# A gated feed-forward block on one core: two down blocks made earlier, one staged tile placed apart, and a set of x sums reordered

## The chip, the cores and the metric

The kernel runs on one core of a Trainium2 chip. The time is device microseconds of that core; the median of three runs before the change is 541.72 us (541.16 to 542.87). The engines are TensorE (PE, with PEld for its weight loads), VectorE (DVE), ScalarE (ACT), GpSimd (POOL) and SyncE (SP), which issues nearly every transfer here, in one queue and in order. One further execution was taken by the profiler: 542.6 us, of which the span from the first to the last instruction is 540.8 us. Places in time below are microseconds from the start of that span.

## What is computed

Input x is 2048 x 1024, w_gate and w_up are 1024 x 3584, w_down is 3584 x 1024, all in bf16:

```python
g = jnp.einsum("bsd,df->bsf", x, w_gate)
u = jnp.einsum("bsd,df->bsf", x, w_up)
h = _gelu(g) * u
return jnp.einsum("bsf,fd->bsd", h, w_down)
```

The kernel doesn't multiply these matrices block by block. It uses a Strassen-like scheme with seven products for eight on 2 x 2 blocks, for the gate and up products and for the down product, and for some units a second level of it. The price is sums and differences of blocks: of x (the t sums), of the weights (the s sums) and of w_down (the "down blocks" m). They are worked out on VectorE, ScalarE and GpSimd beside TensorE's matmuls.

## The kernel before the change

**Passes and units.** The 2048 rows of x are taken in two passes (ip 0 and 1) of 1024. A pass has 14 units, u = 0 to 13, of 256 columns of w_gate and w_up each. Units 1 to 3, 12 and 13 of pass 0 go through `unit` (L238). Units 4 to 11 go two at a time: `pair0` (L357) in pass 0 (a = 4, 6, 8, 10) and `pair1` in pass 1. Behind the units of a pass comes the down stage, `down` (L630).

**Banks.** The eight PSUM banks are four pairs, passed around as roles F, K, E, C. In `unit` the roles are `e, c, d = banks`; in `prepare` and `keep` the pair K is the one that a unit's helper work may use. A product is summed up in a bank by TensorE (L132), copied out by ScalarE (`snap`, L125: u2, p1, p5), and added to others by VectorE (`dve`, L108: sums, "up" sums, then the product of `gelu` (L200) and up, written to hT or hL).

**Order.** The instructions of SP, VectorE, GpSimd and TensorE run in the order of the code, so the order is written by hand; an instruction that waits holds up all behind it on its engine. ScalarE's are in code order within the blocks that a manual schedule marks, which hold the units.

**Rotating places.** `slot` (L97) hands out one of 36 places of 2 KB per partition (kpool) or one of 13 for s sums (spool). wpool has three places of 8 KB for the weight tiles W(u) of a unit and for other big tiles; mpool has two for down blocks (`three`, L100). A new tile in a place waits until all readers of the old one are done, a DMA among them.

**Down blocks.** For each j of 14, three differences of blocks of w_down are made once, in pass 0, stored to DRAM (`store_made`, L534: 768 KB) and loaded in both down stages. Two ways exist. `keep_part` (L512), in three parts: ScalarE casts a piece into a spare bank, VectorE subtracts from it (one bank, one SBUF input). `keep_whole` (L526): three subtractions on GpSimd. Before, `JS` (L62) gives each pair two blocks by parts, ja at its start and jb at its end (blocks 0 to 7); unit 12 makes block 8 and unit 13 block 9 by parts; GpSimd makes 10, 11 (in `prepare` of unit 12), 12 and 13 (of unit 13). `fetch_wd` (L501) loads the raw pieces: two slots for j up to 9, a w place for two blocks from 10 on. The stores of blocks 10 and 11 are issued in unit 13, those of 12 and 13 at the down stage's steps 0 and 2 (`more`, L964).

**The staged outputs.** Nine 512-wide pieces of h in pass 0 have no place yet when they are made, because `forms` lies where hL will be. Eight go to a w place (`staged`, t8), the ninth to a slot named hx (L865). `bring_home` (L346), in pair 10, copies them to hL by two DMAs.

**The x sums of the second level.** `lo_part` (L826) makes T1, T2, T3, T4, TB (in `forms`) from x, in unit 2 for k = 0 and unit 3 for k = 1. Parts 0 to 2 are called in `keep`, part 3 by `turned`, behind the product with s3. While `turned` is set, `unit` adds p5 to the banks of e in place and takes it off again behind the last product (L287).

**The down stage.** `raw[1, n]` holds raw w_down pieces for the first 28 products; four are fetched ahead in unit 13 (L934), the others by the agenda, step by step. Then the stored down blocks follow (`load12`, `load4`).

Of the kernel before, what the change touches and what calls it, by code (L numbers as in the profile page):

```python
# [10 lines left out]
def kernel(  # L11
# [26 lines left out]
    P = nc.NUM_PARTITIONS  # L38
    bf16 = mybir.dt.bfloat16
# [19 lines left out]
    NWARM = 7  # L59
    SLOTS, SUMS = 36, 13  # L60
    FIRST, LAST = 4, 11
    JS = {4: (0, 1), 6: (2, 3), 8: (4, 5), 10: (6, 7)}  # L62
    LAG = 3
    BIG12 = (0, 2, 4)
    AT12 = [6, 6, 10, 10, 14, 14, 16, 18, 20, 22, 27, 29, 31, 33]
# [169 lines left out]
        for i in range(2):  # L235
            nc.scalar.copy(out=ps[i], in_=src[i])

    def unit(u, banks, s, t, late, after_p5, aside, keep, ahead_of_p4, behind_p4, turned):  # L238
        GU = range(2)
        e, c, d = banks  # L240
        aside(-2)
        g, up = late() if late else (None, None)
        aside(-1)
        for i in GU:
            product(e[i], s["s2"][i], t["t2"], False)
        aside(0)
        keep(0, c)
        u2 = [snap(e[i], "u2") for i in GU]
        if late:
            g = gelu(g)  # L250
        c11 = g, up
        keep(1, c)
        keep(2, c)
        c = d
        for i in GU:
            product(c[i], s["s1"][i], t["t1"], True)
        p5 = [snap(c[i], "p5") for i in GU]
        after_p5()
        for i in GU:
            product(e[i], s["s3"][i], t["t3"], False)  # L260
        if turned and u % 2:
            turned(banks[1])
        elif turned:
            g, up = add(e, p5)
            times(2 * u + 1, 1, gelu(g), up)
            turned(banks[1])
        else:
            g, up = new(dve, e[0], p5[0], ADD, "sum", dtype=f32), banks[1][not late]
            dve(up, e[1], p5[1], ADD)
        if late:  # L270
            times(2 * u, 0, *c11)
        for i in GU:
            product(c[i], s["s4"][i], t["tb"], False)
        if not turned:
            times(2 * u + 1, 1, gelu(g), up)
        aside(1)
        g, up = add(c, u2)
        times(2 * u, 1, gelu(g), up)
        if turned and u % 2:
            g, up = add(e, p5)  # L280
            times(2 * u + 1, 1, gelu(g), up)
        ahead_of_p4()
        for i in GU:
            product(e[i], s["sa"][i], t["t4"], False)
        behind_p4()
        if turned:
            dve(e[1], e[1], p5[1], SUB)  # L287
        times(2 * u + 1, 0, gelu(e[0]), e[1])


# [1 line left out]
    T1, T2, T3, T4, TB = [[forms[:, 2 * n + i] for i in range(2)] for n in range(5)]  # L292
    pd = dpool.tile([P, LAST - FIRST + 1, 2, N], f32, name="pd")
    st8 = []

    def staged(n, c):
        if not st8:
# [59 lines left out]
    def pair0(a, roles, S, t, js, hooks):  # L357
# [16 lines left out]
        sb.make("s4")  # L374

        def keep(j, n, ps):
            keep_part(j, n, ps[n % 2])

        ja, jb = js
        hooks("w", n)  # L380
        keep(ja, 0, K)
        full(F, sa["s2"], t["t2"])
# [19 lines left out]
        hadd(E, u2a, 2 * a, 1)  # L402
        part(K, q["r3"], T3, False)
        squared(F, p5a, 2 * a + 1)
        part(E, q["r1"], T1, True)
        sb.make("sa")
        hooks("w", nn)
# [1 line left out]
        full(C, sb["s3"], t["t3"])  # L409
        for i in range(2):  # L410
            dve(A[i], K[i], p5r[i], ADD)
        part(E, q["r4"], TB, False)
        hooks("pd", b)
        part(K, [x[:, H:] for x in sb["s1"]], T4, False)
        hooks("home", b)
        for i in range(2):
            dve(B[i], E[i], u2r[i], ADD)
        hooks("pd", a)
        hooks("fetch", a)
        p5b = [snap(K[i], "p5") for i in range(2)]  # L420
        raw1(F, W(n))
# [78 lines left out]

    def fetch_wd(js):  # L501
        for j in js:
            if j < NJ - 4:
                wraw[j] = [slot([P, Dm], bf16, "raw") for _ in range(2)]
            else:
                if j % 2 == 0:
                    big = wpool.tile([P, 4, Dm], bf16, name="w")
                wraw[j] = [big[:, 2 * (j % 2) + kh] for kh in range(2)]
            for kh in range(2):
                nc.sync.dma_start(out=wraw[j][kh], in_=wdn[:, kh, j, :])  # L510

# [13 lines left out]

    def keep_whole(j):  # L526
        ra, rb = wraw[j]
        made[j] = wpool.tile([P, 4, N], f32r, name="w") if j in (NJ - 3, NJ - 2) else three(f32r)
        m = [made[j][:, n] for n in range(3)]
        pool(m[0], ra[:, N:], ra[:, :N], SUB)  # L530
        pool(m[1], rb[:, N:], m[0], SUB)
        pool(m[2], rb[:, :N], m[1], SUB)
# [265 lines left out]

    def making(u):
        if u == NU - 2:  # L800
            return [8]
        return [9, 10, 11, 12, 13] if u == NU - 1 else []

    E, K, C, F = odd, cc, dd, even
    S, p5 = {}, {}
# [20 lines left out]
    def lo_part(k, part, c):  # L826
        t1 = t["t1"]
        if part == 0:
            nc.scalar.copy(out=c[0], in_=lo[:, KH + k])
            dve(c[0], c[0], lo[:, k], SUB)  # L830
        if part == 1:
            nc.scalar.copy(out=c[1], in_=lo[:, KH + H + k])
            dve(TB[k], c[1], lo[:, H + k], SUB)
            dve(T3[k], TB[k], c[0], SUB)
        if part == 3:
            dve(c[0], c[0], t1[k], SUB)
            dve(c[1], TB[k], c[0], SUB)
            dve(T4[k], t1[H + k], c[1], SUB)
            nc.scalar.copy(out=T1[k], in_=c[0])
            nc.scalar.copy(out=T2[k], in_=c[1])  # L840

# [5 lines left out]
    for ip in range(NPASS):  # L847
        with tc.manual_schedule(engines={ENG.Activation}):
# [6 lines left out]
            for u in range(1 if ip == 0 else 0, NU):  # L855
                if upgraded(u):
                    if u % 2:
                        continue
                    if u == FIRST:
                        S = {u: s, u + 1: sums_s(W(u + 1), pool)}  # L860
                    if (ip, u) == (0, FIRST):
                        for n in range(4):
                            for c in range(2):
                                away[NH + n, c] = lambda n=n, c=c: staged(n, c)
                        away[NH + 4, 0] = lambda: slot([P, N], bf16, "hx")  # L865

                    def hooks(what, n):
                        if what == "w":
                            W(n)
                            if ip == 0 and n - 3 in JS:  # L870
                                fetch_wd(JS[n - 3][1:])
                            if ip and n <= LAST:
                                fetch_p5(n)
                        if what == "home" and n == LAST:
                            bring_home()
                        if what == "pd":
                            k = 0 if n % 2 else KH
                            nc.sync.dma_start(
                                out=pd[:, n - FIRST].rearrange("p i n -> p (i n)"),
                                in_=flat(xT[1][:, k : k + KH]),  # L880
                            )
                        if what == "made":
                            store_made(n)
                        if what == "fetch":
                            fetch_wd(JS.get(n + 2, [8, 10, 11])[: 1 if n + 2 in JS else 3])

                    roles = F, C, K, E
                    if ip == 0:
# [10 lines left out]
                def prepare():  # L899
                    if first:  # L900
                        pool_behind(t["t4"][-1])
                    if u + 1 < NU:
                        nxt["s"] = make_s(W(u + 1), pool, nxt.get("s"))
                    if ip == 0:
                        if js:
                            store_made(js[0])
                        if u == NU - 2:
                            for j in making(u + 1)[1:3]:
                                keep_whole(j)
                        if u == NU - 1:  # L910
                            for j in js[3:]:
                                keep_whole(j)
                        if u == FIRST - 2:
                            fetch_wd(JS[FIRST][:1])

                def keep(part, ps):
                    if js:
                        keep_part(js[0], part, ps[part // 2])
                    if ip == 0 and u in (2, 3):
                        lo_part(u - 2, part, ps)  # L920

                def aside(part):
                    if first and part < 0:
# [5 lines left out]
                        if (ip, u) == (0, 1):  # L929
                            load_lo()  # L930
                    if part == 0 and (ip, u) == (0, NU - 2):
                        fetch_wd([9, 12, 13])
                    if part == 0 and (ip, u) == (0, NU - 1):
                        for n in range(4):  # L934
                            fetch12(n)
                            ahead12.add(n)
                        for j in js[1:3]:
                            store_made(j)
                    if part == 0 and "t4" not in t:
                        t.make("t4")  # L940

# [9 lines left out]
                if u % 2 and not first:  # L951
                    E, K, C = C, E, K
                banks = (E, K, C) if u % 2 else (F, K, E)
                turned = (lambda c: lo_part(u - 2, 3, c)) if ip == 0 and u in (2, 3) else None
                unit(
                    u, banks, s, t, late if first else None, prepare, aside, keep,
                    ahead_of_p4, behind_p4, turned,
                )
                s = nxt.pop("s", None)

# [3 lines left out]
        def more(step):  # L964
            if last:
                return
            if step in (0, 2):
                store_made({0: NJ - 2, 2: NJ - 1}[step])
            if step == 0:
                xT[:] = new_x()  # L970
            if step >= 24 and step % 2 == 0 and step // 2 - 12 < len(moves):
# [43 lines left out]
```

## Time and profile before

| what | value |
|---|---|
| median of three runs | 541.72 us (541.16 to 542.87) |
| the profiled execution | 542.6 us |
| its span | 540.8 us, 7482 instructions |
| granted TensorE clock | 1.000 |
| transfers | 103.91 MB, mean 192 GB/s |
| HBM read, written | 78.64 MB, 19.40 MB |

How to read it: "busy" is the time in which an engine ran instructions, beside its share of the span. A row such as `out<-in xcount` groups instructions by the tiles they write and read. The bracket behind a row of the timeline is the time for which the engine sat idle before it and the instruction or transfer that ended the wait last, inferred from semaphores. SPq rows are the issues of transfers, and their duration is that of issuing, not of moving data. Busy times by stretch (us, then PE, PEld, DVE, ACT, POOL, granted clock, DMA share of 16 engines, GB/s):

```profile
40.00:64.00 24.00, 23.69 (x107) 16.83 (x107) 20.59 (x32) 16.73 (x32) 23.98 (x23) 1.00 0.34 98
64.00:94.00 30.00, 29.93 (x134) 22.05 (x134) 20.86 (x32) 20.86 (x39) 23.59 (x26) 1.00 0.43 132
94.00:122.00 28.00, 27.93 (x126) 20.34 (x126) 20.82 (x33) 20.16 (x38) 23.97 (x25) 1.00 0.69 207
150.00:178.00 28.00, 26.89 (x120) 19.43 (x120) 18.17 (x29) 17.66 (x34) 23.39 (x23) 1.00 0.83 278
178.00:200.00 22.00, 19.89 (x84) 14.99 (x83) 16.65 (x26) 14.27 (x28) 15.31 (x14) 1.00 0.86 307
200.00:226.00 26.00, 25.47 (x116) 11.87 (x118) 21.51 (x33) 2.58 (x6) 2.12 (x2) 1.00 1.12 370
```

The first stretch holds units 2 and 3, the second and third pairs 4 and 6, the fourth pair 10, the fifth units 12 and 13, the last the beginning of the down stage. GpSimd's last instruction of pass 0 is in that last stretch.

### The profile page before, as it was taken

The page shows a single profiled execution, that of the slowest core. Times are in us where ns is not written, and L with a number is a line of the kernel's source. Part 1 is how long each engine was busy: PE and PEld are TensorE (multiplying, and loading weights), DVE is VectorE, ACT ScalarE, POOL GpSimd, SP SyncE. Part 2 cuts the span into 40 slices and gives each one's busy share as a digit, 9 for nine tenths or more (in the row PEclk, how much of TensorE's full clock was granted, in tenths as well). Part 3 has the DMA queues.
Part 4 walks back from the last instruction along what each step waited for, and adds up shares of the span by engine and source line. Part 5 has one row for each costly group of instructions (what it writes and reads, how often), then busy time and mean ns, then how long its engine had stood idle before and what let it go on. Part 6 is the DMA issues. An engine that isn't in the chain of part 4 may idle for free.

```text
span 540.8 us, 7482 instructions
## 1 busy us (share of the span) xinstructions
PE 531.4 (98%) x2372; PEld 377.5 (70%) x2393; DVE 363.4 (67%) x564; ACT 276.2 (51%) x497; POOL 269.0 (50%) x253
## 2 busy tenths in 40 slices
PE   9999999999999999999999999999999999999997
PEld 5568686868686664588886867668667685488886
DVE  2987867777775879658587455576675749775830
ACT  3557676868683741015345645656666551104351
POOL 1079986979798480000006949793979620000000
PEclk9999999999999999999999999999999999999999
DMA  9795063946769799989995443343561239655571
GB/s 245 174 232 167 1 175 117 279 150 196 233 196 320 252 388 365 337 253 216 259 322 151 122 137 99 115 120 113 160 189 28 57 102 383 235 175 161 170 240 53
DMA packets 115527, 103.91 MB, mean 192 GB/s; under 512 B 21792, under 2 KB 97696, under 8 KB 115360
## 3 DMA queue, kind: packets, MB, share of 16 engines
q1 hardware_dynamic: 115488, 103.44, 64.4%
q8 instruction: 19, 0.31, 0.3%
q14 instruction: 20, 0.16, 0.1%
HBM read 78.64 MB, written 19.40 MB: 181 GB/s over the span
## 4 chain that ended last, share of the span: by engine, by line
PE 89%; DMA 4%; DVE 3%; ACT 2%; issue 1%; SPq 0%; DVEq 0%; ACTq 0%
PE bank L132 89%; DMA raw<-in_w_down_dram 2%; DMA hL<-hx 1%; DVE bank L108 1%; DMA xn<-in_x_dram 1%; ACT g L200 1%; DVE hT L108 1%; DVE forms L108 0%; DVE sum L108 0%; DVE m L108 0%; DVE hL L108 0%; ACT bank L519 0%; SPq L707 0%; ACT forms L840 0%; ACT u L125 0%
## 5 line engine op out<-in xcount | busy, mean ns | idle before, releaser
L111 POOL TENSOR_TENSOR s<-w 128x512 fp32r<-128x512 bf16 x102 | 120.2, 1194 | 138.7 <-PE bank L132 107.5
L132 PE MATMUL bank<-t,s 128*128 128x512 f32 x552 | 132.1, 392 | 1.0 <-DVE m L108 0.7
L132 PEld LDWEIGHTS bank<-t,s 128*128 128x128 f32 x552 | 103.5, 188 | 23.9 <-DVE m L108 1.1
L132 PE MATMUL bank<-xT,w 128*128 128x512 bf16 (+1 forms) x489 | 108.0, 376 | 2.3 <-DMA raw<-in_w_down_dram 0.9
L132 PEld LDWEIGHTS <-w 128*128 128x128 bf16 x504 | 47.8, 98 | 60.0 <-issue 6.6
L200 ACT ACTIVATE g<-sum 128x512 f32<-128x512 f32 x81 | 51.5, 635 | 65.9 <-DVE sum L108 60.0
L125 ACT COPY p<-bank 128x512 f32<-128x512 f32 x102 | 57.7, 590 | 50.0 <-PE bank L132 50.0
L108 DVE TENSOR_TENSOR sum<-bank,p 128x512 f32<-128x512 f32 x54 | 37.1, 687 | 38.1 <-PE bank L132 37.0
L108 DVE TENSOR_TENSOR hT<-g,bank 128x512 bf16<-128x512 f32 x72 | 49.1, 687 | 16.3 <-ACT g L200 9.9
L111 POOL TENSOR_TENSOR s<-w,s 128x512 fp32r<-128x512 bf16 x50 | 57.9, 1174 | 0.9 <-PE bank L132 0.6
L111 POOL TENSOR_TENSOR s<-s,w 128x512 fp32r<-128x512 f32 x50 | 57.4, 1164 | 0.4
L132 PE MATMUL bank<-tb,s 128*128 128x512 f32 x216 | 54.4, 394 | 1.2 <-ACT p L125 1.2
L132 PE MATMUL bank<-t,sa 128*128 128x512 f32 x216 | 55.1, 397 | 0.0
L120 ACT CAST tb<-raw 128x512 fp32r<-128x512 bf16 x28 | 17.5, 630 | 73.4 <-PE bank L132 30.3
L108 DVE TENSOR_TENSOR bank<-bank,p 128x512 f32<-128x512 f32 x72 | 49.8, 695 | 7.4 <-PE bank L132 7.4
L132 PE MATMUL bank<-q 128*128 128x512 f32 x208 | 51.7, 389 | 0.0
L132 PEld LDWEIGHTS bank<-tb,s 128*128 128x128 f32 x216 | 40.4, 188 | 10.5 <-POOL w L111 1.5
L132 PEld LDWEIGHTS bank<-t,sa 128*128 128x128 f32 x216 | 40.6, 188 | 9.1
L132 PEld LDWEIGHTS bank<-q 128*128 128x128 f32 x208 | 39.0, 188 | 8.1
L125 ACT COPY u<-bank 128x512 f32<-128x512 f32 x56 | 32.1, 594 | 15.7 <-PE bank L132 15.7
L132 PE MATMUL bank<-raw,hT 128*128 128x512 bf16 x140 | 31.2, 379 | 0.2
L108 DVE TENSOR_TENSOR q<-raw 128x512 fp32r<-128x512 bf16 x28 | 19.2, 687 | 17.9 <-DMA raw<-in_w_down_dram 10.3
(80 smaller groups left out, 636.1 us busy)
## 6 DMA issues: line engine op xcount, KB each, us to landing
raw<-in_w_down_dram SPq DMA_DIRECT2D x72, 256.0 KB, 5.1
w<-in_w_gate_dram SPq DMA_DIRECT2D x27, 512.0 KB, 4.7
w<-in_w_up_dram SPq DMA_DIRECT2D x27, 512.0 KB, 5.9
q<-td SPq DMA_DIRECT2D x52, 256.0 KB, 4.4
td<-m SPq DMA_DIRECT2D x12, 768.0 KB, 5.3
w<-td SPq DMA_DIRECT2D x6, 1024.0 KB, 9.8
pd<-xT SPq DMA_DIRECT2D x8, 512.0 KB, 4.6
out_dram<-st SPq DMA_DIRECT2D x32, 128.0 KB, 1.9
```

Of the source, the lines that this page charges most:

```text
L108: nc.vector.tensor_tensor(out=out, in0=a, in1=b, op=op)
L111: nc.gpsimd.tensor_tensor(out=out, in0=a, in1=b, op=op)
L120: nc.scalar.copy(out=t, in_=src)
L125: nc.scalar.copy(out=t, in_=ps)
L132: nc.tensor.matmul(ps, lhsT=lhs, rhs=rhs, start=start, stop=stop, skip_group_check=True)
L200: nc.scalar.activation(g, src, ACT.Gelu_apprx_tanh)
```

## The change

- `JS` and a new `MID`: pairs 4 and 6 make a third block each, by parts, in their middle (blocks 1 and 4); pairs 8 and 10 make 6, 7 and 8, 9; unit 12 makes 10 and unit 13 makes 11, by parts.
- GpSimd makes 12 and 13 alone, both in `prepare` of unit 12, into w places; their stores are issued in unit 13 and at step 0 of the down stage.
- The raw pieces of blocks 1 and 4 come into one w place, loaded ahead of pair 4; those of 12 and 13 into another, as before.
- hx has a place of its own in xpool.
- In units 2 and 3, parts 0 and 1 of the x sums are both made in the first `keep`, part 2 (three VectorE steps, split off from part 3) in the last, and part 3 (the two copies to T1 and T2) in `prepare`. `turned` is gone from `unit`: the up sum is written to the other bank pair as in other units, and the subtraction behind the last product falls away.

The order of TensorE's instructions is the same in both. VectorE has four instructions more (six block subtractions more, two subtractions less), ScalarE six more, GpSimd six fewer; SP issues the same transfers in another order.

```diff
-    JS = {4: (0, 1), 6: (2, 3), 8: (4, 5), 10: (6, 7)}
+    JS = {4: (0, 2), 6: (3, 5), 8: (6, 7), 10: (8, 9)}
+    MID = {4: 1, 6: 4}
+    BIGS = (1, 4, 12, 13)
...
-        if turned and u % 2:
-            turned(banks[1])
-        elif turned:
-            g, up = add(e, p5)
-            times(2 * u + 1, 1, gelu(g), up)
-            turned(banks[1])
-        else:
-            g, up = new(dve, e[0], p5[0], ADD, "sum", dtype=f32), banks[1][not late]
-            dve(up, e[1], p5[1], ADD)
+        g, up = new(dve, e[0], p5[0], ADD, "sum", dtype=f32), banks[1][not late]
+        dve(up, e[1], p5[1], ADD)
...
-        if turned and u % 2:
-            g, up = add(e, p5)
-            times(2 * u + 1, 1, gelu(g), up)
...
-        if turned:
-            dve(e[1], e[1], p5[1], SUB)
...
+    hx = xpool.tile([P, N], bf16, name="hx")
...
         ja, jb = js
+        jm = MID.get(a)
...
         squared(F, p5a, 2 * a + 1)
+        keep(jm, 0, F)
         part(E, q["r1"], T1, True)
...
             dve(A[i], K[i], p5r[i], ADD)
+        keep(jm, 1, F)
+        keep(jm, 2, F)
         part(E, q["r4"], TB, False)
...
         hooks("pd", a)
+        if jm is not None:
+            hooks("made", jm)
         hooks("fetch", a)
...
-            if j < NJ - 4:
+            if j not in BIGS:
                 wraw[j] = [slot([P, Dm], bf16, "raw") for _ in range(2)]
...
-        made[j] = wpool.tile([P, 4, N], f32r, name="w") if j in (NJ - 3, NJ - 2) else three(f32r)
+        made[j] = wpool.tile([P, 4, N], f32r, name="w")
...
         if u == NU - 2:
-            return [8]
-        return [9, 10, 11, 12, 13] if u == NU - 1 else []
+            return [10]
+        return [11] if u == NU - 1 else []
...
-        if part == 3:
+        if part == 2:
             dve(c[0], c[0], t1[k], SUB)
             dve(c[1], TB[k], c[0], SUB)
             dve(T4[k], t1[H + k], c[1], SUB)
+        if part == 3:
             nc.scalar.copy(out=T1[k], in_=c[0])
             nc.scalar.copy(out=T2[k], in_=c[1])
...
                     if (ip, u) == (0, FIRST):
+                        fetch_wd(MID.values())
...
-                        away[NH + 4, 0] = lambda: slot([P, N], bf16, "hx")
+                        away[NH + 4, 0] = lambda: hx
...
-                            fetch_wd(JS.get(n + 2, [8, 10, 11])[: 1 if n + 2 in JS else 3])
+                            fetch_wd(JS[n + 2][:1] if n + 2 in JS else [10, 12, 13])
...
+                    if ip == 0 and u in (2, 3):
+                        lo_part(u - 2, 3, K)
                     if u + 1 < NU:
                         nxt["s"] = make_s(W(u + 1), pool, nxt.get("s"))
...
-                            for j in making(u + 1)[1:3]:
-                                keep_whole(j)
-                        if u == NU - 1:
-                            for j in js[3:]:
+                            for j in BIGS[2:]:
                                 keep_whole(j)
...
                     if ip == 0 and u in (2, 3):
-                        lo_part(u - 2, part, ps)
+                        for n in ((0, 1), (), (2,))[part]:
+                            lo_part(u - 2, n, ps)
...
-                        fetch_wd([9, 12, 13])
+                        fetch_wd([11])
...
-                        for j in js[1:3]:
-                            store_made(j)
+                        store_made(BIGS[2])
...
-            if step in (0, 2):
-                store_made({0: NJ - 2, 2: NJ - 1}[step])
+            if step == 0:
+                store_made(BIGS[3])
```

More of the change, by code (lines that the diff above doesn't have):

```diff
@@ L236, in into, with unit @@
             nc.scalar.copy(out=ps[i], in_=src[i])
-    def unit(u, banks, s, t, late, after_p5, aside, keep, ahead_of_p4, behind_p4, turned):
+    def unit(u, banks, s, t, late, after_p5, aside, keep, ahead_of_p4, behind_p4):
         GU = range(2)
@@ L273, in unit @@
             product(c[i], s["s4"][i], t["tb"], False)
-        if not turned:
-            times(2 * u + 1, 1, gelu(g), up)
+        times(2 * u + 1, 1, gelu(g), up)
         aside(1)
@@ L278, in unit @@
         times(2 * u, 1, gelu(g), up)
-        if turned and u % 2:
-            g, up = add(e, p5)
-            times(2 * u + 1, 1, gelu(g), up)
         ahead_of_p4()
@@ L376, in keep @@
         def keep(j, n, ps):
-            keep_part(j, n, ps[n % 2])
+            if j is not None:
+                keep_part(j, n, ps[n % 2])
         ja, jb = js
+        jm = MID.get(a)
         hooks("w", n)
@@ L502, in fetch_wd @@
         for j in js:
-            if j < NJ - 4:
+            if j not in BIGS:
                 wraw[j] = [slot([P, Dm], bf16, "raw") for _ in range(2)]
             else:
-                if j % 2 == 0:
+                n = BIGS.index(j) % 2
+                if n == 0:
                     big = wpool.tile([P, 4, Dm], bf16, name="w")
-                wraw[j] = [big[:, 2 * (j % 2) + kh] for kh in range(2)]
+                wraw[j] = [big[:, 2 * n + kh] for kh in range(2)]
             for kh in range(2):
@@ L953 @@
                 banks = (E, K, C) if u % 2 else (F, K, E)
-                turned = (lambda c: lo_part(u - 2, 3, c)) if ip == 0 and u in (2, 3) else None
                 unit(
                     u, banks, s, t, late if first else None, prepare, aside, keep,
-                    ahead_of_p4, behind_p4, turned,
+                    ahead_of_p4, behind_p4,
                 )
```

## The prediction

> **What bounds the kernel now.** I read the clock per core first (1.000 over the whole span, so nothing is throttled), then the page's busy times.
>
> ```profile
> span 540.8 us, 7482 instructions
> PE 531.4 (98%) x2372; PEld 377.5 (70%) x2393; DVE 363.4 (67%) x564; ACT 276.2 (51%) x497; POOL 269.0 (50%) x253
> ```
>
> TensorE is the bound, and the change leaves its instructions and their order as they are. So only its idle time can change: 540.8 - 531.4 = 9.4 us. Of that 3.2 us lie behind the last matmul (it ends at 537.6), 1.25 us in the first 20 us (18.75 busy), and about 1.3 us in gaps of 0.07 us that most stretches of 20 us show alike. The rest is in the waits of TensorE:
>
> ```profile
> PE bank L132 <- DMA raw<-in_w_down_dram: 1.3, 3, 0.9
> PE bank L132 <- ACT p L125: 1.2, 1, 1.2
> PE bank L132 <- DVE m L108: 0.7, 1, 0.7
> PE bank L132 <- ACT u L125: 0.2, 1, 0.2
> PE bank L132 <- DVE hT L108: 0.2, 1, 0.2
> ```
>
> TensorE's timeline tells where they stand (start, duration, and in brackets the idle time before and what ended it):
>
> ```profile
> 63.33 1.02 PE L132 MATMUL bank<-xT,w 128*128 128x512 bf16 x4 [0.24 <-DVE hT L108]
> ...
> 176.00 3.02 PE L132 MATMUL bank<-xT,w 128*128 128x512 bf16 x12 [0.93 <-DMA raw<-in_w_down_dram]
> ...
> 181.59 2.10 PE L132 MATMUL bank<-t,s 128*128 128x512 f32 x8 [0.71 <-DVE m L108]
> 183.94 2.06 PE L132 MATMUL bank<-t,s 128*128 128x512 f32 x8 [0.25 <-ACT u L125]
> ...
> 196.43 2.07 PE L132 MATMUL bank<-tb,s 128*128 128x512 f32 x8 [1.16 <-ACT p L125]
> ...
> 221.26 1.89 PE L132 MATMUL bank<-raw,hL 128*128 128x512 bf16 x7 [0.21 <-DMA raw<-in_w_down_dram]
> ```
>
> With a last one of 0.16 us at 223.31 these are 3.66 us: 0.24 in unit 3, 1.89 between the last pair and unit 12, 1.16 in unit 13, 0.37 where the down stage begins. Behind 230 us TensorE waits for nothing. Four lines of ScalarE and VectorE show what stands behind the middle ones:
>
> ```profile
> 174.59 0.63 ACT L200 ACTIVATE g<-sum 128x512 f32<-128x512 f32 x1 [4.63 <-DMA hL<-hx]
> 175.25 0.69 DVE L108 TENSOR_TENSOR hL<-g,bank 128x512 bf16<-128x512 f32 x1 [3.36 <-ACT g L200]
> 193.94 0.69 DVE L108 TENSOR_TENSOR m<-bank,raw 128x512 fp32r<-128x512 f32 x1 [2.77 <-issue]
> 194.67 1.11 ACT L519 CAST bank<-raw 128x512 f32<-128x512 bf16 x2 [2.34 <-DVE m L108]
> ```
>
> **The change, part by part.** Times of steps are added from rows: a VectorE subtraction or product lasts 0.69 us and starts 0.60 after the one before it, 0.73 if it reads that one's result; ScalarE's gelu lasts 0.63, its copy 0.59, with 0.5 between starts.
>
> *The staged tile (hx).* A gelu output g takes the rotating place that hx had, so ScalarE waits 4.63 us until hx has been copied home. The product of that g ends at 175.25 + 0.69 = 175.94, and TensorE starts at 176.00 in the bank it read: this is the 0.93 (the row names a DMA, but these matmuls read no raw tile). With a place of its own, g follows its sum: VectorE did the second half of that addition at 171.20, so g runs at 171.3 and its product ends at 172.7, well ahead of 175.07, where TensorE would need the bank. Then the rest of the in-order chain: addition 172.65 and 173.25, g 173.4, product 174.1 to 174.8, subtraction to 175.4, product to 176.1, then three block subtractions at 176.1, 177.3 and 178.0, the last ending at 178.7. TensorE, 0.93 earlier, wants that bank at about 179.8 (before: 180.9, and 181.59 when it got it). So 0.71 goes with 1.1 us to spare. Next: sum 178.6, g 179.4, a cast to 180.5, the two u copies to 181.0 and 181.5, wanted at 181.8 and 182.7: 0.25 goes with 0.8 to spare. Together 1.89; bounds: 0 if another wait stands in the same place, 1.89 if none.
>
> *Two down blocks fewer on GpSimd at the end, two more in pairs 4 and 6.* In unit 13 block 9's first subtraction stands 2.77 us behind GpSimd's use of the m buffers and a store that took 7.5 us (issued 186.31); the next cast waits for it (194.67), then the p copies, then TensorE: 1.16. Now unit 13 makes block 11, whose m buffer is freed by the store of block 9, issued as block 9 is done, about 178.8; at 4.3 to 8.2 us for such stores (issues of 181.56 to 190.24) it lands by 187.0. The subtraction would want to start about 189.2. The raw data of block 11 come behind that store: issue 179.2 to 180.5, 4.6 us, landed by 185.1, wanted by ScalarE at 188.3. So 1.16 goes; bounds 0 and 1.16.
>
> GpSimd made four blocks from 185.98 to 202.2, with two waits for m buffers; two blocks of 3.7 us, straight after its last s sum (184.1, now 183.2), end near 190.6. SP's queue stood behind it: the store at 202.22 and then a burst of thirteen transfers. From 200 to 220 the DMA share is 1.03 at 374 GB/s, and the last raw transfer, issued at 212.41, took 10.85 us. Two stores (2 x 768 KB) leave this region, and the one at 202.22 can go out near 194: three stores, 2.3 MB, at 374 GB/s are 6 us of transfers less in it, against TensorE's arrival 3.3 us earlier. So the 0.37 goes too (bounds 0 and 0.37, and a loss, see the rivals).
>
> *Price of the middle blocks.* Six casts on ScalarE (590 ns) and six subtractions on VectorE (690 ns), half in pair 4, half in pair 6, into bank pair F, which is idle between its last product and the next raw product. In pair 4:
>
> ```profile
> 77.74 1.15 ACT L120 CAST sa<-w 128x512 fp32r<-128x512 bf16 x2
> 83.08 1.07 ACT L125 COPY p<-bank 128x512 f32<-128x512 f32 x2 [2.61 <-PE bank L132]
> 78.84 0.69 DVE L108 TENSOR_TENSOR hT<-g,bank 128x512 bf16<-128x512 f32 x1
> 83.51 3.40 PE L132 MATMUL bank<-xT,w 128*128 128x512 bf16 x15
> ```
>
> The first cast goes ahead of the sa casts (77.8), subtraction 79.4; sa casts to 79.4; p5 copies to 80.5; A additions 80.1 and 80.7; casts two and three to 81.6; subtractions 81.3 and 82.0, ending at 82.7. TensorE takes F at 83.51: 0.8 us to spare. VectorE's B additions slip from 82.1 to 82.6, the next sum from 83.7 to 83.8, and the product that follows waited 1.43 us anyhow. I take 0. The cover is this 0.8 us; once it is gone, each further us late costs one in each pair, and the raw product of F, its p1 copies and the unit's sums are late behind it.
>
> Here the Trainium skill speaks against the change. "Perfetto Trace Analysis", section "Optimizing Scalar/DVE Operations", warns that moving work between GpSimd and VectorE might not help, since they share a read port; "SBUF — State Buffer", section "Who interferes with whom", limits this to VectorE instructions with two SBUF inputs. These have one (the other is PSUM), and the row agrees: the block subtraction at 96.84 took 0.68 us inside a GpSimd run from 96.30 to 98.59. By the limited rule and the row the price is 0; by the warning taken broadly it is the third rival's.
>
> *The big tile for blocks 1 and 4* holds one of three w places from 48 us to the middle of pair 6. SP's order puts its four loads ahead of W(6), which now waits for W(4)'s last reader, the raw product ending at 60.7; W(7) waits for the sa casts of pair 4, 79.5 instead of 72.2. Two places are what pair 8 has now, as t8 holds the third:
>
> ```profile
> 134.72 0.37 SPq L142 DMA_DIRECT2D w<-in_w_gate_dram  x1
> ...
> 146.16 3.63 PE L132 MATMUL bank<-xT,w 128*128 128x512 bf16 x16
> ```
>
> Its W(11) goes out 11.4 us ahead of its first matmul, lands 5.3 us after issue, and TensorE doesn't wait. One pair is 27.87 us, so pairs 4 and 6 repeat this some 0.5 us later (the extra cast). GpSimd's s1, s2 of unit 7 end near 90.1, wanted at 97. I take 0, by pair 8; at the slowest landing seen (10.85) W(7) would come at 90.8, wanted at 90.4, and W(9) likewise: bounds 0 and 0.8 lost. The extra store goes out behind the pd stores and delays the next raw fetch by some 2 us of 11.
>
> *x sums in units 2 and 3.* Two subtractions go (2 x 0.69), the T1, T2 copies come ahead of the sa casts, and the up sum goes to the second K bank once T2 is copied. Unit 2: both casts by 41.5, six form steps on VectorE from 41.4 to 45.5, T2 copied at 46.1, e sum 45.4 (before 45.35), up sum 46.2 (46.26), the c sum 48.3 instead of 49.73, as no form step stands ahead of it. Unit 3: casts 50.2 and 50.7, six form steps 51.0 to 55.1, e and up sums 55.0 and 55.6, c sums 57.3 and 57.9, their product to 59.4, then the raw sums at 60.0 and, when the bank is ready, 60.8, gelu to 61.3, product 61.5 to 62.2. Before, the chain was back to back on VectorE to 63.28; TensorE wants that bank at 63.1. So 0.24 goes, with 0.9 to spare at the tightest u2 copy (52.3, wanted at 53.2). Bounds: 0.24 gained to nothing.
>
> **Sum.** 0.24 + 1.89 + 1.16 + 0.37 = 3.66 us, 0 added: 542.6 (the profiled execution, 1.8 us more than its span) becomes 538.9. The median of the runs shown is 541.72, 0.9 below it. If those runs hold the same waits they come to 538.1; if their waits are that much shorter, to 538.9. I take the middle, 538.5.
>
> **Rivals.** (1) The waits don't go but change hands: hx is free, yet the same bank waits for the copies, or unit 13 waits for store 9. For: margins of 0.8 to 1.8 us against stores that vary by 4. Then only about half is won: 541.72 - 1.9 = 539.8, at worst 541. Against: each margin is as large as the wait it replaces.
> (2) The down stage takes it back: TensorE arrives 3.3 us earlier at transfers that land as before, and waits 3.3 more at 219 to 223: 541.7. For: 374 GB/s there. Against: GpSimd's end, 11 us earlier, was what held SP.
> (3) Slower: in pairs 4 and 6 each of three subtractions is blocked by a running GpSimd instruction (1.15 us each), so F is 3.45 - 0.8 = 2.65 us late in each pair, 5.3 in all: 541.72 - 3.66 + 5.3 = 543.4. It decides from 0.8 + 3.66 / 2 = 2.6 us late in each pair on: there the gain is eaten. Against: the 0.68 us row.
>
> **How the numbers follow.** Forecast 0.70, rival 1 0.14, rival 2 0.08, rival 3 0.08. The forecast's own range is 537.3 (538.1 less the runs' 0.8) to 539.6. Rival 1 fills 539.6 to 541; to leave out no more than 2 in 10 the range goes to 541.2. About 0.3% (1.6 us, so 540.1) can be told from no change. Faster: the forecast and two thirds of rival 1, 0.79; same: the rest of rival 1 and most of rival 2, 0.12; slower 0.09.
>
> **What would show it.** No ScalarE row waiting for hL<-hx; no TensorE wait at 170 to 200; GpSimd ending near 188 to 191; the p copies in unit 13 back to back; no TensorE wait at the raw products of F near 83.3 and 111.1. Wrong, if TensorE waits for m or w tiles between 80 and 125, or for raw tiles at 215 to 225, or if the waits left sum to over 1.5 us.

## The result, and the profile after

| what | before | after |
|---|---|---|
| median (six runs each) | 541.87 us (541.16 to 542.87) | 536.78 us (536.68 to 537.70) |
| ratio, 95% interval | | 0.9909 (0.9896 to 0.9922) |
| the profiled execution, its span | 542.6, 540.8 us | 537.0, 535.2 us |
| TensorE's clock | 1.000 | 1.000 |

The change takes 5.1 us off the median and 5.6 us off the profiled execution; 3.66 us were forecast for the latter. First the page of the kernel after: span, busy times, shares of the chain of waits.

```profile
span 535.2 us, 7481 instructions
PE 529.3 (99%) x2372; PEld 377.4 (71%) x2393; DVE 364.9 (68%) x568; ACT 279.8 (52%) x503; POOL 261.4 (49%) x247
PE 98%; DMA 1%; issue 0%; SPq 0%; ACT 0%
```

TensorE's idle time fell by 3.5 us (9.4 to 5.9), close to the 3.66 forecast, but its busy time fell too, by 2.1 us (531.4 to 529.3), with the same 2372 records. That is what the forecast lacked. (In the first 20 us 0.36 us of busy time turned into idle time, and the matmuls behind them start within 0.03 us of where they did.) The list of waits, for TensorE alone (waited for: us in total, times, longest), has only two entries left, both from the first microseconds; none of the seven waits is there, and no new one:

```profile
PE bank L767 <- PEq L997: 0.8, 1, 0.8
PE bank L712 <- DMA xn<-in_x_dram: 0.7, 2, 0.5
```

TensorE's timeline, first two groups before, then after, from pair 10 to the beginning of the down stage:

```profile
174.03 1.04 PE L132 MATMUL bank<-xT,w 128*128 128x512 bf16 x4
...
178.67 2.21 PE L132 MATMUL bank<-t,s 128*128 128x512 f32 x8
```

```profile
173.62 3.63 PE L134 MATMUL bank<-xT,w 128*128 128x512 bf16 x16
176.90 5.84 PE L134 MATMUL bank<-t,s 128*128 128x512 f32 x24
...
191.74 1.98 PE L134 MATMUL bank<-tb,s 128*128 128x512 f32 x8
...
210.92 8.80 PE L134 MATMUL bank<-raw,hL 128*128 128x512 bf16 x39
```

A row without a bracket shows no wait before it. Before, the group that starts at 173.62 began at 174.03, and the one at 176.90 at 178.67: from the one start to the next the stretch is 3.28 us long, not 4.64. That is 1.36 us less, though the bracket said 0.93 (and the single records show 0.11 more at 177.99). So a wait can be priced by the starts on both sides of it. Done for all seven, from the starts of the single matmuls in both traces:

| wait before (us), kind of the matmul that waits | idle shown | start to start | more |
|---|---|---|---|
| 63.33, bf16 | 0.24 | 0.42 | 0.18 |
| 176.00 and 177.99, bf16 | 1.04 | 1.37 | 0.33 |
| 181.59 and 183.94, f32, with 0.11 at 185.95, where no idle time shows | 0.96 | 1.60 | 0.64 |
| 196.43, f32 | 1.16 | 1.41 | 0.25 |
| 221.26 and 223.31, bf16 | 0.37 | 0.69 | 0.32 |
| 276.8, a late weight load | 0 | 0.11 | 0.11 |
| sum | 3.77 | 5.60 | 1.83 |

The sum agrees with the whole difference between the two profiled executions (last matmul 5.59 us earlier). The 0.11 at 276.8 is not the change's: the repeat of the kernel before, below, doesn't have it. Two records show where the surplus hides. The first matmul behind the wait of unit 13 before, and the load of its weights:

```profile
196.43 0.47 PE L132 MATMUL bank<-tb,s 128*128 128x512 f32 x1 [1.16 <-ACT p L125]
```

```profile
196.40 0.19 PEld L132 LDWEIGHTS bank<-tb,s 128*128 128x128 f32 x1 [1.55 <-POOL w L111]
```

In a full stream an f32 matmul starts 227 ns after the one before, but its record lasts 389 ns. When TensorE stops, the last record runs 162 ns past the moment at which the next matmul would have started, and the idle time is counted from there: 0.16 us of each wait stands in the rows as busy. (The profile's own key says that the ends of matmuls are modelled, so the starts are the firmer measure.) Then the weights (0.19 us) are loaded as the first matmul starts, its record is 0.47 long, and the second starts 307 ns behind it: 0.08 us more.

What the forecast's steps look like after, in the timelines of ScalarE, of GpSimd and of SP's issues:

```profile
170.91 0.63 ACT L202 ACTIVATE g<-sum 128x512 f32<-128x512 f32 x1 [1.35 <-DVE sum L110]
...
189.89 1.08 ACT L127 COPY p<-bank 128x512 f32<-128x512 f32 x2
```

```profile
181.65 7.33 POOL L113 TENSOR_TENSOR w<-w 128x512 fp32r<-128x512 bf16 x6
```

```profile
178.18 0.33 SPq L533 DMA_DIRECT2D td<-m  x1
...
191.90 0.89 SPq L533 DMA_DIRECT2D td<-w  x1
```

ScalarE's gelu no longer waits for hx (170.91), and the p copies of unit 13 stand together (189.89). GpSimd's two blocks end at 188.98, and SP's last store of them goes out at 191.90, 10.3 us earlier than this one before:

```profile
202.22 0.32 SPq L535 DMA_DIRECT2D td<-m  x1
```

### The profile page after: what moved, and what is told of

Same layout as the page of the kernel before. It is cut to its first block, busy times and chain, and to the rows that moved or that the text cites. A ratio compares the mean times of both kernels' runs of the same rounds, so it can differ in the third digit from the quotient of the medians.

```text
span 535.2 us, 7481 instructions
## 1 busy us (share of the span) xinstructions
PE 529.3 (99%) x2372; PEld 377.4 (71%) x2393; DVE 364.9 (68%) x568; ACT 279.8 (52%) x503; POOL 261.4 (49%) x247
## 4 chain that ended last, share of the span: by engine, by line
PE 98%; DMA 1%; issue 0%; SPq 0%; ACT 0%
PE bank L134 98%; DMA xn<-in_x_dram 1%; SPq L705 0%; PE bank L712 0%; ACT st L677 0%
## 5 line engine op out<-in xcount | busy, mean ns | idle before, releaser
L110 DVE TENSOR_TENSOR bank<-bank,p 128x512 f32<-128x512 f32 x70 | 48.5, 696 | 7.0 <-PE bank L134 6.8
```

Of the source, the lines that this page charges most:

```text
L110: nc.vector.tensor_tensor(out=out, in0=a, in1=b, op=op)
```

## The experiments

"Hidden price" is the theory read from the two traces: a wait costs its shown idle time and a further fixed amount that the rows count as busy. Its rivals: the idle time shown is all, and the other 1.9 us come from elsewhere (fewer GpSimd instructions, a better rate of the matmuls); or the waits change hands.

**The parts alone.** The kernel before with one part of the change each, and the changed kernel with one part undone.

```diff
# e1_hx, on the kernel before
+    hx = xpool.tile([P, N], bf16, name="hx")
-                        away[NH + 4, 0] = lambda: slot([P, N], bf16, "hx")
+                        away[NH + 4, 0] = lambda: hx
# e2_xsums, on the kernel before: the edits of lo_part, keep, prepare and unit alone
# e3_blocks, on the kernel before: JS, MID, BIGS and all that goes with them alone
```

> The kernel before with only the place of its own for hx. Its three waits between pair 10 and unit 12 (0.93, 0.71, 0.25, idle time 1.89 us) should be gone from TensorE's rows. Theory 'hidden price' (each wait costs its shown idle time and 0.25 to 0.28 us more, which stands in the rows as busy time): 1.89 + 3 x 0.27 = 2.7 us less, 539.0 to 539.3, and TensorE's busy time about 0.8 us lower with the same matmuls. Rival 'idle as shown' (the rest of the gain has another source, such as fewer GpSimd blocks): 1.89 us less, 539.9, busy time unchanged. Rival 'waits change hands': the waits of unit 13 and of the down stage grow by up to 1.9 us, and the time is 541 or more.

> The kernel before with only the x sums of units 2 and 3 moved. One wait of 0.24 us. 'Hidden price': 0.40 to 0.5 us less (541.3 to 541.4 against 541.8). 'Idle as shown': 0.24 less (541.5). If the waits behind change hands: 0.

> The kernel before with only the down blocks moved (two more by parts in pairs 4 and 6, two fewer on GpSimd); hx stays in a rotating place and the x sums as before. Waits of 1.16, 0.21 and 0.16 us should go, those around hx stay. 'Hidden price': 1.53 + 3 x 0.27 = 2.3 us less, 539.4 to 539.6. 'Idle as shown', with the rest of the gain out of fewer GpSimd instructions and a better rate of the matmuls: 1.53 + 1.9 = 3.4 us less here, 538.4, and none of the 1.9 in the run with hx alone. If the middle blocks cost time in pairs 4 and 6 it is above 540.3.

| run | median | ratio to before (median 541.58) |
|---|---|---|
| e1_hx | 539.65 us | 0.9957 (0.9944 to 0.9969) |
| e2_xsums | 541.16 us | 0.9991 (0.9982 to 1.0000) |
| e3_blocks | 539.72 us | 0.9964 (0.9952 to 0.9976) |

The medians alone do not decide: 1.9 us for hx is what "idle as shown" said, and its interval reaches to 3.0. The rows do. TensorE in e1_hx:

```profile
174.41 3.63 PE L132 MATMUL bank<-xT,w 128*128 128x512 bf16 x16
177.68 5.87 PE L132 MATMUL bank<-t,s 128*128 128x512 f32 x24
...
193.66 2.09 PE L132 MATMUL bank<-tb,s 128*128 128x512 f32 x8 [0.99 <-ACT p L125]
...
220.49 1.89 PE L132 MATMUL bank<-raw,hL 128*128 128x512 bf16 x8 [0.15 <-DMA raw<-in_w_down_dram]
```

The stretch between the first two starts is 3.27 us instead of 4.64, with GpSimd's work as before: the surplus does not come from the blocks. The wait of unit 13 stays (0.99 against 1.16) and so do those of the down stage (0.13 and 0.15 against 0.21 and 0.16): nothing changes hands. Start to start, the waits around hx gave back 2.98 us for 2.00 shown. e2_xsums lost the one wait of unit 3: 0.42 for 0.24 shown. TensorE in e3_blocks:

```profile
174.07 4.12 PE L134 MATMUL bank<-xT,w 128*128 128x512 bf16 x16
177.84 2.19 PE L134 MATMUL bank<-t,s 128*128 128x512 f32 x8
180.76 2.11 PE L134 MATMUL bank<-t,s 128*128 128x512 f32 x8 [0.73 <-DVE m L110]
183.12 2.08 PE L134 MATMUL bank<-t,s 128*128 128x512 f32 x8 [0.24 <-ACT u L127]
...
213.50 8.80 PE L134 MATMUL bank<-raw,hL 128*128 128x512 bf16 x40
```

The waits of unit 13 and of the down stage are gone (1.41 and 0.69 start to start, for 1.16 and 0.37), and no 1.9 us beside them, so fewer GpSimd instructions speed up no matmul. One thing no theory had expected: with hx in its rotating place the first wait (0.93 before) had shrunk to 0.06, while the second and third stood as before. The next two runs ask why.

**How firm the first wait is.**

> The kernel before once more, to see how much its waits differ from one execution to the next. The copy of hx home landed 6.3, 6.0 and 5.4 us after its issue ended in the three profiles that have hx in a rotating place, and TensorE's first wait behind it was 0.93, 0.59 and 0.06 us. 'The landing differs from run to run': the first wait lies anywhere from 0 to 1 us here, the second and third stay at 0.71 and 0.25, the one of unit 13 at 1.0 to 1.2, and the time follows the first wait (540.9 to 542.7). 'The first wait belongs to the order of the instructions': it is 0.93 again.

> The changed kernel with hx back in a rotating place, and nothing else undone. The three waits come back: 0 to 0.93, 0.71 and 0.25 us shown. 'Hidden price by kind' (0.16 for the first, bf16, 0.25 to 0.3 for the other two, f32): 0.96 + 0.55 = 1.5 us over the changed kernel without the first wait, 2.6 with 0.93 of it: 538.3 to 539.4. 'Idle as shown': 537.7 to 538.7. If hx's place does not matter in the changed kernel, 536.8.

e9_before_again took 542.58 us; e10_hx_back has a median of 539.22, a ratio of 0.9959 (0.9945 to 0.9972) to before, 2.4 us over the changed kernel. TensorE and ScalarE in e9_before_again, then in e10_hx_back:

```profile
176.82 3.02 PE L132 MATMUL bank<-xT,w 128*128 128x512 bf16 x12 [1.26 <-DVE hL L108]
```

```profile
175.42 0.63 ACT L200 ACTIVATE g<-sum 128x512 f32<-128x512 f32 x1 [4.97 <-DMA hL<-hx]
```

```profile
174.77 3.02 PE L134 MATMUL bank<-xT,w 128*128 128x512 bf16 x12 [0.27 <-DVE hL L110]
...
180.37 2.12 PE L134 MATMUL bank<-t,s 128*128 128x512 f32 x8 [0.74 <-DVE m L110]
182.72 2.09 PE L134 MATMUL bank<-t,s 128*128 128x512 f32 x8 [0.24 <-ACT u L127]
```

```profile
173.37 0.63 ACT L202 ACTIVATE g<-sum 128x512 f32<-128x512 f32 x1 [3.98 <-DMA hL<-hx]
```

The same kernel before shows 0.93 in one execution and 1.26 in another; over the five profiles with hx in a rotating place the first wait is 0.93, 0.59, 0.06, 1.26 and 0.27, as the copy home lands (TensorE restarts 1.40 us behind the start of the gelu that the copy holds up, in all five), and the other two are always 0.71 to 0.74 and 0.24 to 0.25. Two expectations for the repeat failed: the first wait lies above 0 to 1, and the wait of unit 13 was 0.86, below 1.0 to 1.2. Nor does the time follow the first wait. It is that of the first execution: what the repeat lost by this wait and in its first 50 us (0.34 and 0.48 us) it has less at unit 13 (0.29) and at the beginning of the down stage (0.53, no wait there). So the first wait may be a part of why the runs before spread over 1.7 us and the profiled one lay 0.7 above the median, but that is not shown; the runs of e1_hx, which has no such wait in its profile, spread over 1.3 us. In e10 1.36 us of idle came back (0.27, 0.11, 0.74, 0.24), and 2.33 us start to start; its median lies in the range of "hidden price" (538.3 to 539.4) and above that of "idle as shown" (537.7 to 538.7).

**The price of a wait by itself.** Waits put into the second pass of the changed kernel: a VectorE instruction that reads the bank which TensorE has just filled and writes what the next group needs.

```diff
# e5, e6, e7 (64 columns, 512, twice 512): in unit, and ahead of full(C, sb["s2"]) in pair1
+            dve(c[0][:, :512], e[1][:, :512], t["t1"][0][:, :512], SUB)
...
+            dve(t["t2"][0][:, :512], xT[1][:, KH, :512], t["t1"][0][:, :512], SUB)
# e8: in pair1, ahead of squared(F) and of hadd(E)
+        dve(K[0], F[1], t["t1"][0], SUB)
...
+        dve(F[0], E[1], t["t1"][0], SUB)
```

> The changed kernel with a made wait ahead of ten groups of f32 matmuls in the second pass: a VectorE subtraction of 64 columns that can start only when the group before is done and that the next group needs (in six units the whole group before must be done, in four pairs all but its last three matmuls). What VectorE writes is overwritten or the same value, so the outputs stay. Bounds for the subtraction itself: 0 to 0.69 us. 'Hidden price by kind' (a wait costs its shown idle time, and 0.16 us because the last matmul's row outlasts the distance to the next start, and for f32 0.08 to 0.13 more because the first weights are loaded late): start to start each of the six loses its shown idle + 0.24 to 0.29 us; the four in pairs lose nothing or up to 0.3. 'Idle as shown': no more than the idle shown.

> The same with 512 columns (0.69 us). Shown idle about 0.8 us in the six units, 0 to 0.2 in the four pairs. 'Hidden price by kind': 0.24 to 0.29 more for each wait, so about 6 x 1.07 + 4 x 0.3 = 7.6 us over the changed kernel (544.4). 'Idle as shown': 6 x 0.8 + 4 x 0.1 = 5.2 (542.0). 'In proportion' (the hidden part grows with the wait): as 0.28 on 1.0.

> The same with two subtractions of 512 columns in a row, each wait 0.6 to 0.73 us longer: 1.5 us shown in the units, 0.7 in the pairs. 'Hidden price by kind': again 0.24 to 0.29 more each, about 6 x 1.77 + 4 x 0.97 = 14.5 us over the changed kernel (551.3). 'Idle as shown': 11.8 (548.6). 'In proportion': 0.4 hidden in each wait of the units.

> The changed kernel with a made wait of one subtraction of 512 columns ahead of eight groups of bf16 matmuls in the second pass (the raw products of the four pairs). Shown idle about 0.8 us each, or more where VectorE is late. 'Hidden price by kind': 0.14 to 0.18 us more for each, start to start, as bf16 weights load in half the time of f32 ones; the first matmul's row has its usual length. 'One price for all': 0.24 to 0.29 more. 'Idle as shown': nothing more.

| run | median | idle of one wait, shown | start to start less shown |
|---|---|---|---|
| e5_f32_64 | 553.84 us (548.52 to 554.96) | 0.20 to 1.00 (nine waits), 4.88 (one) | 0.26 to 0.30 |
| e6_f32_512 | 552.31 us (551.84 to 558.61) | 0.84 to 1.47 (ten) | 0.26 to 0.31 |
| e7_f32_1024 | 572.22 us (571.05 to 578.12) | 2.14 to 2.66 (ten) | 0.26 to 0.31 where the clock holds at the restart (four) |
| e8_bf16_512 | 544.96 us | 0.79 to 0.80 (eight) | 0.144 to 0.160 |

The last two columns are read from one profiled execution of each (553.88, 552.17, 578.12 and 545.07 us). The totals of e6 and e7 were expected far too low (544.4 and 551.3), since the made waits were longer than set out (VectorE starts only behind ScalarE's u copies, and its subtractions in the pairs took 1.06 to 1.53 us instead of 0.69), and e7 lost clock besides (last section). The price itself came out as "hidden price by kind" had it: the same for 0.2 us of idle as for 2.6, so not in proportion, and about half for bf16. The first matmul behind a wait, in e6_f32_512 and in e8_bf16_512:

```profile
293.32 0.50 PE L134 MATMUL bank<-t,s 128*128 128x512 f32 x1 [1.41 <-DVE bank L110]
```

```profile
354.36 0.38 PE L134 MATMUL bank<-xT,w 128*128 128x512 bf16 x1 [0.79 <-DVE bank L110]
```

The bf16 record has its usual length and the next starts 215 ns later, as in a full stream: only the 0.16 us of the record before the wait are hidden. The f32 one is 0.11 longer. In e8, 8 x (0.79 + 0.15) = 7.5 of the 8.2 us over the changed kernel are the waits; most of the rest lies in the first 40 us, where the two executions of the kernel before differ as much.

**The margin of the middle blocks.** In pairs 4 and 6 their second and third step were done twice.

```diff
         keep(jm, 1, F)
         keep(jm, 2, F)
+        keep(jm, 1, F)
+        keep(jm, 2, F)
```

> The changed kernel with the second and third step of each middle block done twice (two casts and two subtractions more in pair 4 and in pair 6). Bank F, ready 0.5 us ahead of its raw product in the changed kernel (82.36 against 82.88), is then ready at about 83.7, so TensorE should wait in both pairs. 'Hidden price': 0.65 us shown and 0.9 lost in each, 1.8 us in all, 538.6 against 536.8. 'Idle as shown': 1.3 in all, 538.1. If TensorE does not wait there, the margin is larger than read, and the time stays 536.8; if the third rival's blocking by GpSimd shows, subtractions last over 1 us and the loss is above 3 us.

539.67 us, 0.9958 (0.9946 to 0.9971) of before, 2.9 us over the changed kernel. VectorE and TensorE in pair 4 of the changed kernel, then of e4_mid_twice:

```profile
80.88 1.48 DVE L110 TENSOR_TENSOR m<-bank,m 128x512 fp32r<-128x512 f32 x2
```

```profile
82.88 3.63 PE L134 MATMUL bank<-xT,w 128*128 128x512 bf16 x15
```

```profile
81.19 3.07 DVE L110 TENSOR_TENSOR m<-bank,m 128x512 fp32r<-128x512 f32 x4
```

```profile
84.32 3.61 PE L134 MATMUL bank<-xT,w 128*128 128x512 bf16 x16 [0.96 <-DVE m L110]
```

So the margin is real and small: the bank is ready at 82.36, 0.5 us ahead of TensorE, and 1.6 us of further subtractions make a wait of 0.96 in pair 4 and 0.98 in pair 6, 1.10 and 1.12 start to start. The expectation had 0.65 and 0.9: each added cast waits for the subtraction that frees its bank, so the chain is longer than two steps at 0.6. The profiled execution (540.1) is 3.1 us over that of the changed kernel: 2.2 us in the pairs, 0.5 at 274, where a weight load came late, and 0.3 in the first 40 us. No subtraction took over 0.7 us.

## Why the prediction was wrong in size and right in kind

**The step that failed** is the size of the terms in the sum: "0.24 + 1.89 + 1.16 + 0.37 = 3.66 us, 0 added". Each term took the bracketed idle time as the price of its wait. Start to start the same waits, with the 0.11 at 177.99 and the 0.11 at 185.95, cost 0.42 + 2.97 + 1.41 + 0.69 = 5.49 us: 0.16 to 0.18 us more than shown for each bf16 wait, 0.22 to 0.30 for each f32 one. With those prices the profiled execution comes to 542.6 - 5.49 = 537.1 (measured 537.0). The median, reckoned from the two ends that the prediction used, comes to the middle of 541.72 - 5.49 = 536.2 and 537.1, so 536.7 (forecast 538.5, measured 536.78).

**The accounting of idle time** was wrong beside it. "About 1.3 us in gaps of 0.07 us" are no gaps: the profiles of before and after lack 21 matmul records of 2393 (weight loads are complete, x2393), and where one is missing its neighbours seem 0.05 to 0.07 us apart. The ten other profiles have all 2393 records and no such row of gaps. So these gaps are missing records, and busy times of profiles with different counts must not be compared. The forecast took nothing from these gaps, so this error cost it nothing.

**hx.** Right, step by step: gelu at 170.91 (forecast 171.3, on a time scale 0.4 later), the last block subtraction ends at 178.16 (178.7), the u copies start at 179.84. The margins came out smaller than forecast, 0.8 us for the first bank instead of 1.1, because TensorE came earlier than the idle time let expect.

**Unit 13 and the down stage.** Right, and rival 1 falls, since no wait took the place of another: the store of block 9 went out at 178.18 (178.8), the p copies stand back to back, GpSimd ended at 188.98 (190.6), the store came at 191.90 (near 194), and TensorE does not wait at 210 to 223, where 334 GB/s flow from 200 to 226. Rival 2 falls: e1_hx brought TensorE 2.7 us earlier to the down stage with the old order of stores, and the waits there did not grow.

**Middle blocks, w place, x sums.** The middle blocks and the w place cost nothing, as forecast. W(7) was issued at 79.22 (79.5); GpSimd waited 6.66 us for it and had the sums of unit 7 near 90.9 (90.1), in time. Bank F had 0.5 us to spare in pair 4 (0.8). The 0.24 of the x sums went too: the product that held TensorE up in unit 3 now ends at 62.12 (62.2), and TensorE takes its bank at 62.95 (63.1) without a wait. In pair 4 the subtractions met no running GpSimd instruction at all, since GpSimd stood in that wait. In pair 6 one did, in the changed kernel:

```profile
106.92 0.68 DVE L110 TENSOR_TENSOR m<-bank,w 128x512 fp32r<-128x512 f32 x1
```

```profile
105.75 2.32 POOL L113 TENSOR_TENSOR s<-s,w 128x512 fp32r<-128x512 f32 x2
```

It took 0.68 us: rival 3 falls. Its counterpart is in e5_f32_64, where the subtraction has two SBUF inputs:

```profile
391.92 5.10 DVE L110 TENSOR_TENSOR t<-xT,t 128x64 fp32r<-128x64 bf16 x1
```

```profile
391.31 4.51 POOL L113 TENSOR_TENSOR s<-w 128x512 fp32r<-128x512 bf16 x4
```

64 columns took 5.10 us beside a GpSimd run. The three others of the kind in that execution took 0.42 to 1.06 us, and all four end 0.08 us behind the end of a GpSimd instruction. With one input in PSUM, 64 columns took 0.23 us at 331.04 of the same execution, inside a GpSimd run from 330.34 to 332.64. The Trainium skill ("SBUF — State Buffer", "Who interferes with whom") draws this line, and both sides of it are measured here.

**The median.** 538.1 to 538.9 was spanned because the profiled run lay 0.9 us above the median. Why it lay there stays open: the first wait at hx varies between executions, but the repeat, at 542.58 us, shows that other waits vary against it. Five of the six runs after lie within 0.3 us, the sixth 0.7 above them; whether that comes of hx is not shown.

## What to carry to other kernels

Price a wait of the bounding engine by the starts on both sides of it in a stream that is otherwise full, not by the idle time in the bracket: the records of TensorE's matmuls overlap, so each wait here cost a fixed amount more, and many short waits are worth more than they look. Before trusting a sum of idle time, count the records: many small gaps of one size can be missing ones. A wait behind a transfer can differ from run to run (0.06 to 1.26 us here); take its range from several profiles.

## What the runs showed of the hardware

Behind long waits TensorE also lost its clock. Windows of e7_f32_1024 (us, then busy times of PE, PEld, DVE, ACT, POOL, granted clock, DMA share, GB/s), and two of its waits of the same length:

```profile
293.00:295.20 2.20, 0.10 (x1) 0.00 (x0) 1.40 (x2) 0.58 (x1) 1.54 (x2) 1.00 1.01 241
295.20:298.65 3.45, 3.41 (x8) 2.73 (x9) 0.00 (x0) 0.58 (x1) 1.17 (x1) 0.51 0.02 5
298.65:302.00 3.35, 3.35 (x16) 2.74 (x16) 1.73 (x3) 2.26 (x4) 3.00 (x3) 1.00 0.03 7
```

```profile
295.24 5.50 PE L134 MATMUL bank<-t,s 128*128 128x512 f32 x16 [2.14 <-DVE bank L110]
...
466.36 3.96 PE L134 MATMUL bank<-t,s 128*128 128x512 f32 x16 [2.15 <-DVE bank L110]
```

With 2.14 us of idle the clock was at half for the next 3.41 us, and eight matmuls ran where sixteen do; 16 matmuls took 5.50 us instead of 3.96, about 1.5 us more. Eight of the ten waits of 2.14 to 2.66 us brought such a drop (one of 6.83 us), the two at 466 and 478 none. The drops of one length start at whole multiples of 3.41 us from each other (295.24, 308.89, 329.37, 343.02), from 0.6 us before the restart to 1.5 us after it, so it looks as if fixed stretches of 3.41 us are judged; that was not tried further. The wait of 4.88 us in e5_f32_64 had one too; of the waits up to 1.47 us in the profiled executions none cost clock. (One execution of e6 without a profile took 558.61 us at a mean clock of 0.994; why isn't known.) The Trainium skill ("TensorE: Matmul & The Clock Gate", "HAM oscillation — how this bites in real kernels") warns of idle gaps over about 3.4 us; here 2.1 us were enough, though not each time. The kernel's own waits (up to 1.26 us) cost no clock.
